# Attention and top-choice expert routing on one core: maxima over experts by pairwise trees, first loads tile by tile on two queues, batch 0's columns as even and odd halves

## The chip, the core and the metric

The kernel runs on one core of a Trainium2 chip. The metric is device time in microseconds (us); the median of several runs counts. Engines are named as the profile names them: PE is TensorE (with PEld, its weight loads), DVE is VectorE, ACT is ScalarE, POOL is GpSimd, and SP is SyncE, which here only issues transfers.

## What is computed

Four batches of `q`, `k`, `v` with 5056 tokens of 256 columns go through an attention over columns, and every output token then goes through one of eight experts.

```python
def _attn_ref(q, k, v, tau):                      # q, k, v: 4 x 5056 x 256
    qn = q / (np.linalg.norm(q, axis=1, keepdims=True) + 1e-06)
    kn = k / (np.linalg.norm(k, axis=1, keepdims=True) + 1e-06)
    s = kn.transpose(0, 2, 1) @ qn / tau          # 256 x 256 for each batch
    s = s - s.max(-1, keepdims=True)
    a = np.exp(s)
    a /= a.sum(-1, keepdims=True) + 1e-09
    return (v @ a).astype(np.float32)

def _moe_ref(x, w_gate, w1, w2):                  # x: 20224 x 256, 8 experts
    cap = N // E                                  # 2528 tokens for each expert
    logits = x @ w_gate
    order = np.argsort(-logits.flatten())
    for idx in order:                             # greedy: best (token, expert) pair first
        tok, e = (int(idx) // E, int(idx) % E)
        if assigned[tok] >= 0 or counts[e] >= cap:
            continue
        assigned[tok] = e
        counts[e] += 1
    for e in range(E):
        mask = assigned == e
        out[mask] = np.maximum(x[mask] @ w1[e], 0.0) @ w2[e]
```

## The kernel before, in words

It has two halves. In the first, for each batch `b`, `scores` (L312) streams `k` and `q` in half chunks of 512 tokens (four token tiles of 128, 512 KB of `k` and as much of `q`) into a ring of four buffers named `ua`. PE adds up `k^T q` over the tokens in one PSUM bank (L338; the trace shows two PE instructions for each of these float32 matmuls), ACT squares each half chunk (L343, L347) and DVE adds the squares (L348). All these loads go through SP's queue; a load waits until PE and ACT are through with the buffer. The very first half chunk is loaded in two pieces for each of `k` and `q`: token tile 0, then tiles 1 to 3 (L323). The constants of the router and `tau` come through ACT's queue (`load_consts`, L485).

After the scores of a batch come its lengths, its softmax (DVE, into `ac`), a transpose (`turned_a`) and `gates` (L427): 16 router columns (2 blocks of 8 experts) are worked out on PE and copied by ACT from PSUM into `ac` (L433), ACT copies `ac` to the buffer from which the value product reads (L436), and DVE copies the 16 columns to a small padded tile `g` (`pads`, L439), from which `logits` (L445) reads its weights. These run between the score matmuls of the next batch. Batch 0 is treated apart: its `ac` is split into a high part `a_hi` (float32r, L436, trace name `a_last`) and a low part `a_f[0]` (L438, trace name `a`), and `value` with `x_tiles_0` (L291, L302) multiplies tokens by both, three float32r matmuls for each 128-row block, 264 columns wide (256 outputs and 8 router columns) in four chunks out of five and 256 wide in the last. There the right-hand operand is read as consecutive columns. The products of batches 1 and 3 are plain float32 matmuls (`x_tiles`, L261). Those of batch 2 are cut into high and low parts again (`x_tiles_cut`, L572, and the feed-forward layers L1489 and L1526): there each right-hand operand lies as all even columns and then all odd columns, and is read alternately from the two halves, `p a m -> p m a`, so that the result keeps its order.

In the second half a small planner writes the order of the instructions of each engine by hand. It keeps a modelled clock for PE and for DVE; the routing of each expert (`route`, L596) is a generator that yields a modelled cost ahead of each instruction, and the planner takes up the next one whose modelled time has come, between the main work's own instructions. The order so made is fixed in the program. `route(p, R)` starts with a maximum of the logits over the `R` experts left (L610, a DVE reduction over a transposed view of `L`, 160 columns for each expert), turns it into a sort key, marks where the maximum stands (L630, L632) and takes a second maximum over the codes of the marks, in bfloat16 (L635). Then it searches a threshold in eight rounds (`compare` L711, `totals` L676 and L689, `hits` L696) in which DVE and PE take turns, and `compact` with `listed` makes the list of the tokens. While the first expert is routed, PE multiplies the values of batches 1 to 3 (the string `TURNS`: F is two plain pairs of token tiles, C is one cut half chunk), then eight late pairs, then the first layer of the first expert. `tend` (L1561) is called behind each pair; once the modelled clock is past the landing of the first expert's weights it hands out one of eight pieces (`split_piece`, ACT L1237 and DVE L1240) in which these weights are split into high and low parts. The split parts go into `ua` buffers, some of which have held cut values until then (`PLACES`, `cleave`).

The feed-forward half then runs `layer1` (PE L1489, ACT L1493, DVE L1498 for the low part `hL` of the hidden layer) and `layer2` (PE L1526, ACT L1535, POOL scatter L1537) expert by expert, with the routing of the next expert woven in.

Of the kernel before, what the change touches and what calls it, by code (L numbers as in the profile page):

```python
# [8 lines left out]
F32 = mybir.dt.float32  # L9
F32R = mybir.dt.float32r  # L10
BF = mybir.dt.bfloat16
# [3 lines left out]
AF = mybir.ActivationFunctionType  # L15
OP = mybir.AluOpType
AX = mybir.AxisListType
# [3 lines left out]
B, N, C = 4, 5056, 256  # L21
E, F = 8, 1024
# [6 lines left out]
COLS = B * NCH * T  # L29
# [4 lines left out]
GW = C + E  # L34
# [8 lines left out]
TH = 4  # L43
# [28 lines left out]
TURNS = "FFCFCFCFCFCFCFCFCFFCFC"  # L72
PLACES = ("ub0", "ub1", "ua0", "ua1", "ub0", "ub1", "vr", "ua0", "ua1", "ua2")
BEHIND = {3: "FF", 4: "C", 5: "CC", 6: "FFFF", 7: "CCC", 8: "CCCC", 9: "FFFFFF"}
CUT = (4, 4, 4, 4, 4)
FIRST_CUT = (2, 4, 4, 4, 4, 2)
PE_TO_DVE = 340
# [26 lines left out]
def attention_moe(ctx: ExitStack, tc: tile.TileContext, q, k, vt, tau, wg, w1t, w2t, tabs, out):  # L104
    nc = tc.nc
    V = nc.vector
    S = nc.scalar
# [56 lines left out]
    for lag in range(2):  # L164
        x = const.tile([128, 1], I32, name=f"px{lag}")
# [37 lines left out]
    L = state.tile([128, E, COLS], F32, name="L0")  # L203
# [31 lines left out]
    a_f = [(apool_l if b == 2 else apool).tile([128, 2, GW], F32 if b else F32R, name=f"a{b}") for b in range(B - 1)]  # L235
    a_hi = apool_l.tile([128, 2, GW], F32R, name="a_last")
    vs = {}
    px_at = [0, True]

    def next_px():  # L240
        px_at[0] += 1
# [31 lines left out]
    with ExitStack() as sctx:  # L273
# [17 lines left out]
        def x_tiles_0(c, t, xs, width):  # L291
            n = 2 if width == C else 1
            px = next_px()
            for i in range(t, t + n):
                y = v_two[c, i - i % 2]
                out_ = px[:, (i - t) * C:(i - t) * C + width]
                j = 0
                for kb in range(2):
                    vH, vL = y[:, 0, kb, i % 2, :], y[:, 1, kb, i % 2, :]
                    aH, aL = a_hi[:, kb, 0:width], a_f[0][:, kb, 0:width]  # L300
                    for l, r in ((vH, aH), (vH, aL), (vL, aH)):
                        newest[0] = PE.matmul(out_, lhsT=l, rhs=r, start=(j == 0), stop=(j == 5))  # L302
                        j += 1
            S.activation(xs[:, t % TH:t % TH + n, 0:width], px[:, 0:n * width].rearrange("p (t c) -> p t c", t=n), AF.Copy)

        pads = []
# [5 lines left out]
        def scores(b, extra):  # L312
            sb = ps_s.tile([128, 512], F32, name="s")
            acc_k = wk.tile([128, TH, C], F32, name="acc_k")
            acc_q = wk.tile([128, TH, C], F32, name="acc_q")
            for c in range(NCH):
                n0 = c * CH
                for h in range(T // TH):
                    kq = big("ua").rearrange("p (a t c) -> p a t c", a=2, t=TH)
                    kt, qt = kq[:, 0], kq[:, 1]  # L320
                    first = c == 0 and h == 0
                    last = c == NCH - 1 and h == T // TH - 1
                    for t0, t1 in ((0, 1), (1, TH)) if b + c + h == 0 else ((0, TH),):  # L323
                        for t_, src in ((kt, k), (qt, q)):
                            if c < NCH - 1:
                                rows = src[b, n0:n0 + CH].rearrange("(p t) c -> p t c", t=T)
                                nc.sync.dma_start(t_[:, t0:t1], rows[:, h * TH + t0:h * TH + t1])
                            elif not last:
                                nc.sync.dma_start(t_, src[b, n0:n0 + HALF_CH].rearrange("(p t) c -> p t c", t=TH))
                            else:  # L330
                                n1 = n0 + HALF_CH
                                n2 = n1 + 128 * (TH - 1)
                                nc.sync.dma_start(t_[:, 0:TH - 1], src[b, n1:n2].rearrange("(p t) c -> p t c", t=TH - 1))
                                nc.sync.dma_start(t_[:REST, TH - 1], src[b, n2:n2 + REST])
                    for t in range(TH):
                        np_ = REST if last and t == TH - 1 else 128
                        for ib in range(2):
                            newest[0] = PE.matmul(sb[:, ib * C:(ib + 1) * C], lhsT=kt[:np_, t, ib * 128:(ib + 1) * 128],  # L338
                                                  rhs=qt[:np_, t, :], start=(first and t == 0 and ib == 0),
                                                  stop=(last and t == TH - 1 and ib == 1))  # L340
                    for t_, acc in ((kt, acc_k), (qt, acc_q)):
                        if first:
                            S.activation(acc, t_, AF.Square)  # L343
                        else:
                            sq = wk.tile([128, TH, C], F32, name="sq", bufs=2)
                            for n, t0, t1 in ((128, 0, TH - 1), (REST, TH - 1, TH)) if last else ((128, 0, TH),):
                                S.activation(sq[:n, t0:t1], t_[:n, t0:t1], AF.Square)  # L347
                                V.tensor_tensor(acc[:n, t0:t1], acc[:n, t0:t1], sq[:n, t0:t1], op=OP.add)  # L348
                    if h == 0:
                        for fn in extra.get((c, "half"), ()):  # L350
                            fn()
                for fn in extra.get(c, ()):
                    fn()
            for acc in (acc_k, acc_q):
                V.tensor_tensor(acc[:, 0:2], acc[:, 0:2], acc[:, 2:4], op=OP.add)
                V.tensor_tensor(acc[:, 0], acc[:, 0], acc[:, 1], op=OP.add)
            pn = pcnt.tile([128, 512], F32, name="pc")
            for i, (acc, ib) in enumerate(((acc_k, 0), (acc_k, 1), (acc_q, 0), (acc_q, 1))):
                newest[0] = PE.matmul(pn[:, i:i + 1], lhsT=acc[:, 0, ib * 128:(ib + 1) * 128], rhs=ones_f[:, 0:1],
                                      start=True, stop=True)  # L360
            nrm = wk.tile([128, 4], F32, name="nrm", bufs=2)
            V.tensor_copy(nrm, pn[:, 0:4])
            return sb, nrm
# [63 lines left out]
        def gates(b, ac, aT):  # L427
            pg = ps_m.tile([128, 512], F32, name="pm")
            for ib in range(2):
                for jb in range(2):  # L430
                    PE.matmul(pg[:, ib * E:(ib + 1) * E], lhsT=aT[:, jb, ib * 128:(ib + 1) * 128],
                              rhs=wg_t[:, jb, :], start=(jb == 0), stop=(jb == 1))
            S.activation(ac[:, :, C:GW], pg[:, 0:2 * E].rearrange("p (i e) -> p i e", i=2), AF.Copy)  # L433
            if b == B - 1:
                a_f.append(apool_l.tile([128, 2, GW], F32, name="a_last"))
            S.activation(a_f[b] if b else a_hi, ac, AF.Copy)  # L436
            if b == 0:
                V.tensor_tensor(a_f[0], ac, a_hi.bitcast(F32), op=OP.subtract)  # L438
            V.tensor_copy(pads[b % 2][:, :, 0:E], ac[:, :, C:GW])  # L439

        def late(fn, *args):
            with tc.issue_after(newest[0].ins):
# [136 lines left out]
    def rtile(name, shape=(128, COLS), dt=F32, bufs=None):  # L579
        t = rt.tile(list(shape), dt, name=name, bufs=bufs)  # L580
        return t

    def ve(n, rate=1, psum=False, ptr=0):
        return "V", ((120 if psum else 58) + n / rate) / 0.96 + 66 * ptr
# [8 lines left out]

    done = {}

    def route(p, R):  # L596
        nonlocal L, L2, U01, asg, ne, ne2
        r = {}
# [7 lines left out]
            es = ne[:, 1, 0:1]  # L606
        else:
            m = rtile("m")
            yield ve(R * COLS)
            V.tensor_reduce(m, L[:, 0:R].rearrange("p r c -> p c r"), axis=AX.X, op=OP.max)  # L610
            key = rtile("t1").bitcast(I32)
            yield ve(COLS, 2)
            V.tensor_scalar(key.bitcast(F32), m, 0.0, None, op0=OP.add)
# [8 lines left out]
            hi = rtile("hi", dt=I16)  # L622
# [2 lines left out]
            klo = rtile("klo", dt=I32)  # L625
            yield ve(COLS, 2)
            V.tensor_scalar(klo, key, 0xffff, None, op0=OP.bitwise_and)
            eq = rtile("eq", (128, E, COLS), BF)
            yield ve(R * COLS)
            V.tensor_tensor(eq[:, 0:R], L[:, 0:R], m[:, None, :].to_broadcast([128, R, COLS]), op=OP.is_equal)  # L630
            yield ve(R * COLS)
            V.tensor_tensor(eq[:, 0:R], eq[:, 0:R], code9[:, 0:R, None].to_broadcast([128, R, COLS]), op=OP.mult)  # L632
            f = rtile("f")
            yield ve(R * COLS)
            V.tensor_reduce(f, eq[:, 0:R].rearrange("p r c -> p c r"), axis=AX.X, op=OP.max)  # L635
            yield ve(COLS)
            V.tensor_tensor(f, f, U01, op=OP.mult)
            Q = R + R % 2
# [143 lines left out]
            t1 = rtile("t1")  # L782
# [50 lines left out]
        if R > 1:  # L833
# [23 lines left out]
            L, L2, ne, ne2 = L2, L, ne2, ne  # L857
# [318 lines left out]
    o = Order()  # L1176
# [371 lines left out]
    with tc.manual_schedule():  # L1548
        o.dve = FIRST_LAT
        plan()  # L1550
        cut_w = [None]
# [8 lines left out]

        def tend():  # L1561
            settle()
            if cut_w[0] and o.pe > cut_w[0][0] and len(cut_w[0]) > 1:
                split_piece(0, *cut_w[0].pop(1))

        def pair(b, c, t):
# [9 lines left out]
        past = ""  # L1576
# [5 lines left out]
        for kind in TURNS:  # L1582
# [8 lines left out]
            else:  # L1591
                k = past.count("C")
                b, c, h = cloven[k]
# [37 lines left out]
        for p in range(E):  # L1631
# [32 lines left out]
            h = {}  # L1664
# [98 lines left out]
```

## Time and profile before

| | us |
|---|---|
| median of 3 runs | 1224.33 (1223.97 to 1225.0) |
| the profiled execution | 1227.58 |
| its span on the core | 1225.6 |
| PE busy | 1201.0 (98%) |
| PE weight loads busy | 1096.6 (89%) |
| DVE busy | 870.0 (71%) |
| ACT busy | 581.0 (47%) |
| POOL busy | 408.0 (33%) |

A row of the timeline gives the start, the time from the start of its first instruction to the end of its last, the engine and line, output and inputs, how often, and in brackets the idle time of the engine ahead of it with what ended it. Matmuls overlap: one lasts far longer than the distance to the next, so the distance is read from rows that hold many. A row of a list of waits gives who waited on whom, the sum, how many times, and the longest. A row of the windows gives, for a stretch, each engine's busy time and how many instructions, then the granted PE clock, the DMA engines' busy share and what they moved in GB/s. A row of the chain gives the start, the time, and what stood on the chain.

### The profile page before, as it was taken

The page shows a single profiled execution, that of the slowest core. Times are in us where ns is not written, and L with a number is a line of the kernel's source. Part 1 is how long each engine was busy: PE and PEld are TensorE (multiplying, and loading weights), DVE is VectorE, ACT ScalarE, POOL GpSimd, SP SyncE. Part 2 cuts the span into 40 slices and gives each one's busy share as a digit, 9 for nine tenths or more (in the row PEclk, how much of TensorE's full clock was granted, in tenths as well). Part 3 has the DMA queues.
Part 4 walks back from the last instruction along what each step waited for, and adds up shares of the span by engine and source line. Part 5 has one row for each costly group of instructions (what it writes and reads, how often), then busy time and mean ns, then how long its engine had stood idle before and what let it go on. Part 6 is the DMA issues. An engine that isn't in the chain of part 4 may idle for free.

```text
span 1225.6 us, 23691 instructions
## 1 busy us (share of the span) xinstructions
PE 1201.0 (98%) x8885; PEld 1096.6 (89%) x8885; DVE 870.0 (71%) x2410; ACT 581.0 (47%) x1322; POOL 408.0 (33%) x655
## 2 busy tenths in 40 slices
PE   7999999999999999999999999999999999999997
PEld 6889977798899989899988999999999999999997
DVE  6688696789888878888888888797765453444430
ACT  5657644555434443345354454354455544344331
POOL 1000001110442462344434444444444444443422
PEclk9999999999999999999999999999999999999999
DMA  8998996795333122313422243243234233422310
GB/s 298 354 401 307 405 318 213 171 241 207 121 103 120 58 93 74 134 57 116 147 81 83 75 152 113 82 131 128 86 108 159 86 116 124 142 94 98 103 65 34
DMA packets 69970, 183.82 MB, mean 150 GB/s; under 512 B 11104, under 2 KB 33760, under 8 KB 65248
## 3 DMA queue, kind: packets, MB, share of 16 engines
q1 hardware_dynamic: 39808, 97.54, 22.3%
q0 software_dynamic: 20656, 63.72, 17.6%
q10 hardware_dynamic: 9392, 21.06, 4.5%
q8 instruction: 69, 1.13, 0.4%
q14 instruction: 45, 0.37, 0.1%
HBM read 122.77 MB, written 59.24 MB: 149 GB/s over the span
## 4 chain that ended last, share of the span: by engine, by line
PE 83%; DVE 8%; issue 4%; POOL 2%; DMA 1%; ACT 1%; POOLq 0%; another core or an unknown queue 0%; SPq 0%; DVEq 0%; ACTq 0%
PE ph L1489 31%; PE py L1526 29%; PE s L338 9%; PE px L261 4%; PE pc L676 3%; PE px L302 2%; PE px L572 2%; PE px L450 1%; POOL out_dram L1537 1%; DVE acc_q L348 1%; DVE acc_k L348 1%; DMA ua<-in_q_dram 1%; DVE ge L711 0%; PE pi L916 0%; DVE f L635 0%
## 5 line engine op out<-in xcount | busy, mean ns | idle before, releaser
L1526 PE MATMUL py<-ua,hH 128*128 128x256 f32 (+1 forms) x2560 | 438.7, 277 | 0.0
L1489 PE MATMUL ph<-xH,ua 128*128 128x512 f32 (+3 forms) x1312 | 394.4, 376 | 3.7 <-DVE hL L1498 3.6
L1526 PEld LDWEIGHTS py<-ua,hH 128*128 128x128 f32 (+1 forms) x2560 | 389.5, 190 | 1.7
L1526 PE MATMUL py<-ua,hL 128*128 128x256 f32 (+1 forms) x1280 | 352.7, 276 | 0.0
L1498 DVE SCALAR_TENSOR_TENSOR hL<-ph,hH 128x512 fp32r<-128x512 f32 (+3 forms) x328 | 217.1, 664 | 109.3 <-ACT hH L1493 97.6
L1493 ACT ACTIVATE hH<-ph 128x512 fp32r<-128x512 f32 (+3 forms) x328 | 191.0, 583 | 202.1 <-PE ph L1489 188.1
L1489 PEld LDWEIGHTS ph<-xH,ua 128*128 128x128 f32 x1312 | 244.8, 189 | 34.6 <-DVE hL L1498 6.2
L1537 POOL DMA_INDIRECT out_dram<-y,idx x160 | 164.4, 1027 | 294.7 <-ACT y L1535 248.2
L1489 PE MATMUL ph<-xL,ua 128*128 128x512 f32 (+3 forms) x656 | 245.4, 374 | 0.5 <-DVE xL L1431 0.5
L1526 PEld LDWEIGHTS py<-ua,hL 128*128 128x128 f32 (+1 forms) x1280 | 243.9, 191 | 0.0
L1259 POOL DMA_INDIRECT xg<-x_d,src x160 | 164.0, 1025 | 93.1 <-issue 52.7
L1535 ACT ACTIVATE y<-py 128x256 f32<-128x256 f32 (+1 forms) x160 | 61.5, 385 | 261.8 <-PE py L1526 204.3
L338 PE MATMUL s<-ua 128*128 128x256 f32 (+1 forms) x640 | 144.9, 385 | 7.1 <-DMA ua<-in_q_dram 7.1
L338 PEld LDWEIGHTS s<-ua 128*128 128x128 f32 (+1 forms) x640 | 121.7, 193 | 26.8 <-issue 6.7
L1489 PEld LDWEIGHTS ph<-xL,ua 128*128 128x128 f32 x656 | 124.2, 189 | 14.6 <-DVE xL L1431 1.5
L347 ACT ACTIVATE sq<-ua 128x1024 f32<-128x1024 f32 (+1 forms) x80 | 76.4, 970 | 51.3 <-DMA ua<-in_k_dram 17.1
L1357 DVE TENSOR_TENSOR xL<-xT,xH 128x256 fp32r<-128x256 f32 (+1 forms) x136 | 50.5, 420 | 58.2 <-ACT xH L1353 57.8
L1270 POOL COPY spacer<-hH 1x1 f32<-1x1 f32 x110 | 24.1, 219 | 158.9 <-ACT hH L1493 148.9
L368 POOL TENSOR_SCALAR ny<-ny 128x4 f32<-128x4 f32 x4 | 2.0, 506 | 182.6 <-ACT ny L367 182.6
L1240 DVE TENSOR_TENSOR ua<-ub,ua 128x512 fp32r<-128x512 f32 x64 | 47.1, 745 | 13.6 <-ACT ua L1237 12.7
L1353 ACT ACTIVATE xH<-xT 128x256 fp32r<-128x256 f32 (+1 forms) x136 | 52.3, 449 | 3.2 <-DMA xT<-via 2.9
L348 DVE TENSOR_TENSOR acc_k<-acc_k,sq 128x1024 f32<-128x1024 f32 (+2 forms) x40 | 44.2, 1112 | 7.9 <-ACT sq L347 6.7
(337 smaller groups left out, 1424.5 us busy)
## 6 DMA issues: line engine op xcount, KB each, us to landing
x_d<-xs ACTq DMA_DIRECT2D x40, 512.0 KB
ua<-in_k_dram SPq DMA_DIRECT2D x35, 512.0 KB
ua<-in_q_dram SPq DMA_DIRECT2D x35, 512.0 KB
via<-xs SPq DMA_DIRECT2D x33, 512.0 KB
xT<-via SPq DMA_DIRECT2D x132, 128.0 KB
vr<-in_vt_dram SPq DMA_DIRECT2D x14, 1024.0 KB
ua<-in_vt_dram SPq DMA_DIRECT2D x4, 1024.0 KB
ua<-in_vt_dram POOLq DMA_DIRECT2D x5, 512.0 KB
```

Of the source, the lines that this page charges most:

```text
L338: newest[0] = PE.matmul(sb[:, ib * C:(ib + 1) * C], lhsT=kt[:np_, t, ib * 128:(ib + 1) * 128], rhs=qt[:np_, t, :], start=(first and t == 0 ...
L347: S.activation(sq[:n, t0:t1], t_[:n, t0:t1], AF.Square)
L348: V.tensor_tensor(acc[:n, t0:t1], acc[:n, t0:t1], sq[:n, t0:t1], op=OP.add)
L1259: P.indirect_dma_start(out=xg[:n, i, :], out_offset=None, in_=rows, in_offset=bass.IndirectOffsetOnAxis(ap=routed[p]["src", col][:n, col:c ...
L1353: S.activation(hi[:, a], rows[:, a], AF.Copy)
L1357: V.tensor_tensor(lo[:, a], rows[:, a], hi[:, a].bitcast(F32), op=OP.subtract)
L1489: PE.matmul(ph[:, 0:nt], lhsT=l[:, w], rhs=in_turn(x_, kb, nt).rearrange("p a m -> p m a"), start=(i == 0), stop=(i == 5))
L1493: S.activation(hH[:, fb, 0:nt], ph[:, 0:nt], AF.Relu)
L1498: V.scalar_tensor_tensor(hL[:, fb, 0:nt], ph[:, 0:nt], 0.0, hH[:, fb, 0:nt].bitcast(F32), op0=OP.max, op1=OP.subtract)
L1526: PE.matmul(py[:n, 0:C], lhsT=l[:, fb, tk], rhs=w, start=(j == 0), stop=(j == 23))
L1535: S.activation(y[:n], py[:n, 0:C], AF.Copy)
L1537: sd = P.indirect_dma_start(out=out, out_offset=bass.IndirectOffsetOnAxis(ap=routed[p]["idx", col][:n, col:col + 1], axis=0), in_=y[:n], i ...
```

## The change

1. The two maxima over the experts in `route` become trees of pairwise maxima (`largest`): the upper half of the experts against the lower half, then again, an odd one taken along in an instruction of its own. Each instruction is its own step for the planner.
2. The first half chunk is loaded token tile by token tile, `k` by SP's queue and `q` by ACT's.
3. Batch 0's high and low parts are written as even and odd columns (`apart`) and read alternately.
4. ACT copies the router columns to `pads` straight from PSUM, ahead of its copy of `ac`; DVE's copy is gone.
5. `tend` hands out a piece of the first expert's first weight only when nine cut half chunks are past, of its second when ten are (`FREED`).

```diff
+FREED = (9, 10)
+    def apart(a):
+        return a.rearrange("p k c -> p (k c)").rearrange("p (a k m) -> p a k m", a=2, k=2)
@@ x_tiles_0
-                    aH, aL = a_hi[:, kb, 0:width], a_f[0][:, kb, 0:width]
+                    aH, aL = (apart(a)[:, :, kb, 0:width // 2].rearrange("p a m -> p m a") for a in (a_hi, a_f[0]))
@@ scores
-                    for t0, t1 in ((0, 1), (1, TH)) if b + c + h == 0 else ((0, TH),):
+                    at_head = b + c + h == 0
+                    for t0, t1 in [(t, t + 1) for t in range(TH)] if at_head else ((0, TH),):
                         for t_, src in ((kt, k), (qt, q)):
                             if c < NCH - 1:
-                                nc.sync.dma_start(t_[:, t0:t1], rows[:, h * TH + t0:h * TH + t1])
+                                (nc.scalar if at_head and src is q else nc.sync).dma_start(t_[:, t0:t1], rows[:, h * TH + t0:h * TH + t1])
@@ gates
-            S.activation(ac[:, :, C:GW], pg[:, 0:2 * E].rearrange("p (i e) -> p i e", i=2), AF.Copy)
+            for to in (ac[:, :, C:GW], pads[b % 2][:, :, 0:E]):
+                S.activation(to, pg[:, 0:2 * E].rearrange("p (i e) -> p i e", i=2), AF.Copy)
-            S.activation(a_f[b] if b else a_hi, ac, AF.Copy)
             if b == 0:
-                V.tensor_tensor(a_f[0], ac, a_hi.bitcast(F32), op=OP.subtract)
-            V.tensor_copy(pads[b % 2][:, :, 0:E], ac[:, :, C:GW])
+                hi, lo = (apart(a).rearrange("p a k m -> p k m a") for a in (a_hi, a_f[0]))
+                in_turn_ = ac.rearrange("p k (m a) -> p k m a", a=2)
+                S.activation(hi, in_turn_, AF.Copy)
+                V.tensor_tensor(lo, in_turn_, hi.bitcast(F32), op=OP.subtract)
+            else:
+                S.activation(a_f[b], ac, AF.Copy)
+    def largest(to, x, tmp, n):
+        while n > 1:
+            h = n // 2
+            yield ve(h * COLS)
+            V.tensor_tensor(to[:, None] if n == 2 else tmp[:, 0:h], x[:, 0:h], x[:, n - h:n], op=OP.max)
+            if n % 2:
+                yield ve(COLS)
+                V.tensor_tensor(to if n == 3 else tmp[:, 0], tmp[:, 0], x[:, h], op=OP.max)
+            x, n = tmp, h
@@ route
-            yield ve(R * COLS)
-            V.tensor_reduce(m, L[:, 0:R].rearrange("p r c -> p c r"), axis=AX.X, op=OP.max)
+            eq = rtile("eq", (128, E, COLS), BF)
+            yield from largest(m, L, eq.bitcast(F32).rearrange("p r c -> p (r c)").rearrange("p (r c) -> p r c", c=COLS), R)
-            eq = rtile("eq", (128, E, COLS), BF)
-            yield ve(R * COLS)
-            V.tensor_reduce(f, eq[:, 0:R].rearrange("p r c -> p c r"), axis=AX.X, op=OP.max)
+            yield from largest(f, eq, eq, R)
@@ tend
-            if cut_w[0] and o.pe > cut_w[0][0] and len(cut_w[0]) > 1:
+            if cut_w[0] and o.pe > cut_w[0][0] and len(cut_w[0]) > 1 and past.count("C") >= FREED[cut_w[0][1][0]]:
                 split_piece(0, *cut_w[0].pop(1))
```

## Rows read from the trace of the kernel before

**Rows 1.** The page: busy time, share of the span and instructions of each engine.
```profile
PE 1201.0 (98%) x8885; PEld 1096.6 (89%) x8885; DVE 870.0 (71%) x2410; ACT 581.0 (47%) x1322; POOL 408.0 (33%) x655
```
**Rows 2.** What PE waited for between 400 and 700 us.
```profile
PE ph L1489 <- DVE hL L1498: 3.6, 3, 1.3
```
**Rows 3.** Timeline of PE, the first 45 us: the score matmuls of batch 0.
```profile
4.08 2.05 PE L338 MATMUL s<-ua 128*128 128x256 f32 x4 [4.08 <-DMA ua<-in_q_dram]
9.12 35.71 PE L338 MATMUL s<-ua 128*128 128x256 f32 x156 [2.99 <-DMA ua<-in_q_dram]
```
**Rows 4.** Timeline of all engines, the first 20 us: constants, second half chunk, buffers freed.
```profile
5.92 0.17 DVE L488 RECIPROCAL scale<-tau_t 128x2 f32<-128x2 f32 x1 [4.24 <-DMA tau_t<-in_tau_dram]
...
11.40 1.23 DVE L348 TENSOR_TENSOR acc_k<-acc_k,sq 128x1024 f32<-128x1024 f32 x1 [2.26 <-ACT sq L347]
11.59 1.06 ACT L347 ACTIVATE sq<-ua 128x1024 f32<-128x1024 f32 x1
...
13.64 0.33 SPq L327 DMA_DIRECT2D ua<-in_k_dram  x1
...
17.09 0.33 SPq L327 DMA_DIRECT2D ua<-in_k_dram  x1
```
**Rows 5.** Windows of the head: all engines, then PE clock, DMA share, GB/s.
```profile
3.50:4.00 0.50, 0.00 (x0) 0.00 (x0) 0.00 (x0) 0.00 (x0) 0.30 (x1) 1.00 0.05 0
...
9.00:10.00 1.00, 0.88 (x2) 0.82 (x3) 0.14 (x2) 0.93 (x1) 0.00 (x0) 1.00 1.05 430
```
**Rows 6.** The chain: runs of matmuls, consecutive columns (L302) and alternating halves (L1526).
```profile
97.57 5.82 PE px L302 x48
...
136.63 5.61 PE px L302 x48
...
988.41 10.72 PE py L1526 x96
```
**Rows 7.** Timeline around batch 0's gates: high part (ACT), low part (DVE).
```profile
81.63 0.65 ACT L436 ACTIVATE a_last<-ac 128x528 fp32r<-128x528 f32 x1
...
83.05 0.70 DVE L438 TENSOR_TENSOR a<-ac,a_last 128x528 fp32r<-128x528 f32 x1
```
**Rows 8.** Timeline at the end of batch 2: when transfers land, when PE comes to batch 3.
```profile
146.94 1.06 ACT L347 ACTIVATE sq<-ua 128x1024 f32<-128x1024 f32 x1 [0.70 <-DMA ua<-in_q_dram]
...
151.08 1.11 PE L338 MATMUL s<-ua 128*128 128x256 f32 x4
```
**Rows 9.** Timeline of batch 3's gates: ACT's copy, DVE's copy, PE's wait.
```profile
215.50 0.18 ACT L433 ACTIVATE ac<-pm 128x16 f32<-128x16 f32 x1 [0.36 <-PE pm L431]
...
217.26 0.13 DVE L439 COPY g<-ac 128x16 f32<-128x16 f32 x1
...
217.59 0.67 PE L261 MATMUL px<-a_last,ua 128*128 128x256 f32 x2 [1.16 <-DVE g L439]
```
**Rows 10.** Timeline of three reductions over experts, and PE's next waits on DVE.
```profile
292.69 2.11 DVE L610 TENSOR_REDUCE m<-L 128x160 f32<-128x1120 f32 x1
...
297.01 0.59 PE L916 MATMUL pi<-E__97,G 128*128 128x162 bf16 x6 [0.55 <-DVE G L906]
...
410.09 1.84 DVE L635 TENSOR_REDUCE f<-eq 128x160 f32<-128x960 bf16 x1
...
415.45 0.36 PE L1489 MATMUL ph<-xH,ua 128*128 128x224 f32 x1 [1.29 <-DVE hL L1498]
...
515.22 1.52 DVE L610 TENSOR_REDUCE m<-L 128x160 f32<-128x800 f32 x1
...
517.33 0.38 PE L916 MATMUL pt<-E__97,G 128*128 128x162 bf16 x3 [1.46 <-DVE ext L1031]
```
**Rows 11.** Timeline of two-operand DVE instructions: float32, and 16-bit in and out.
```profile
236.29 1.48 DVE L711 TENSOR_TENSOR ge<-hi,th 128x1200 bf16<-128x1200 int16 x2
...
278.50 0.32 DVE L786 TENSOR_TENSOR asg<-asg,Gf 128x160 f32<-128x160 f32 x1
```
**Rows 12.** Timeline: the first expert's weights are split, fifth of eight pieces.
```profile
301.74 0.69 ACT L1237 ACTIVATE ua<-ub 128x512 fp32r<-128x512 f32 x1 [0.96 <-PE px L572]
```

## The prediction

> **What bounds the kernel now.** I read the busy shares first: PE works 98% of the span and no other engine over 71% [rows 1]. PE's order is fixed in the program, so a part of the change is worth what it takes out of PE: idle time in which PE waits, or matmuls that come too slowly. Then I read PE's waits stretch by stretch, the timeline around each, and the chain. What PE loses lies in a few places. At the head, PE does token tile 0 at 4.08 and then stands for 2.99 us until `q` of tiles 1 to 3 has landed [rows 3]. Behind that pause it is also slow: the rest of the first half chunk, 12 instructions from 9.12 to the issue at 13.64 that waits for its buffer, takes 4.52 us, while the 16 of the next take 17.09 - 13.64 = 3.45 us, 0.216 each [rows 3, 4]. So 1.9 us (4.52 - 12 x 0.216) go to matmuls at nearly half pace behind idle time, though the granted clock reads 1.00, the upper level (2.4 GHz), in that stretch [rows 5]. In batch 3's gates PE stands 1.16 us for DVE's small copy [rows 9]. Between 290 and 520 us it stands 0.55, 1.29 and 1.46 us for DVE work that came behind a reduction over experts [rows 10]; its waits on `hL` from 400 to 700 are 3.6 us in three [rows 2]. Elsewhere it streams, so time is won only by a denser stream.
>
> **Part by part.**
>
> *First loads.* PE no longer waits for three tiles at once. What ends last next is the second half chunk: ACT begins to square its `q` at 11.59 without waiting for a transfer, so it had landed by then [rows 4]. If it lands as before and PE is through with the first half chunk by then, PE ends the second at 11.59 + 3.45 = 15.04 instead of 17.09: 2.05 us gained. PE has the time: from 4.08, 16 instructions at 0.216 and the 1.9 us of slow start end at 9.4 if tiles come in time, and by 11.3 with 1.9 us more. Bounds: at best the second half chunk lands by 9.4, and 17.09 - (9.4 + 3.45) gives 4.2. At worst PE stands so long ahead of 11.59 that it starts slowly again: 2.05 - 1.9 gives 0.15. The DMA engines moved nothing from 3.5 to 4.0 and 430 GB/s at full share from 9 [rows 5], so there is room for earlier bytes, but I have no row of four loads at once and take 2.0. A later first tile (three more 128 KB pieces beside it are 0.79 MB for `k` and `q`, 1.8 us at 430 GB/s) would only eat slack ahead of 11.59. On ACT's queue the four issues stand ahead of those of the constants, at 0.33 us each (an SP issue in [rows 4]) some 1.3 us. DVE waits for `tau` until 5.92 and has 2.26 us of idle time before its first sum at 11.40 [rows 4]; that covers it, and without the cover ACT's squares would come late, not PE. Behind 17 us PE sets the pace of the loads (each waits for its buffer), so the gain is kept.
>
> A rule of the Trainium skill speaks against the second queue (DMA: Bandwidth & Descriptors, section "Issuing engines are not separate DMA queues"): transfers from several engines share the same 16 DMA engines, and a second issuing engine saves only issue time. By it the bytes come as before and the sum keeps the 2.0; without it, it would have the 4.2.
>
> *Even and odd columns.* `x_tiles_0` has 240 matmuls: 192 of 264 columns at 5.82/48 = 0.1213 us and 48 of 256 at 5.61/48 = 0.1169. The second layer, read alternately, does 256 columns in 10.72/96 = 0.1117 [rows 6]; eight columns more in proportion make 0.1152. The gain is 192 x 0.0061 + 48 x 0.0052 = 1.4 us if batch 0 follows. Its halves lie 1056 bytes apart, not 1024 as elsewhere; if that matters, nothing is gained. I take 1.4, the row of the same reading. Loads hide behind PE in this stage: a transfer that ACT squares at 146.94 belongs to batch 3, which PE begins at 151.08 [rows 8]; 4.1 us of slack against 1.4. Without it the transfers would keep the 1.4.
>
> Against this stands the note on SBUF "cachelines" (the Trainium skill, SBUF — State Buffer, section "Door 1"): accesses that stay in a 16-byte line run at full bandwidth, and each step to another line pays. By it alternating halves is the slow way. The trace disagrees: the alternating run is the faster [rows 6].
>
> *Batch 0's gates.* One more ACT copy, 0.18 us [rows 9], stands ahead of the high part. That ended at 81.63 + 0.65 = 82.28, and DVE was busy until 83.05 before the low part [rows 7], so 0.77 us cover the copy and a slower strided write. Without the cover it costs 0.2. I take 0.
>
> *Batch 3's router columns.* ACT's copy into `g` follows the one at 215.50 and ends near 215.9 instead of 217.26 + 0.13 = 217.39 [rows 9]. PE's wait of 1.16 goes; the copy of the whole of `a`, which now starts 0.18 later, may stand last for that matmul instead. I take 1.0, bounds 0.5 to 1.2. For batches 1 and 2 nobody waited on that copy: 0.
>
> *Trees.* Two-operand float32 instructions take 0.32 us for 160 elements and 1.23 for 1024 [rows 4, 11]: 0.15 + 1.05 ns for each element. For seven experts the tree is 480, 160, 160, 160: 0.65 + 3 x 0.32 = 1.61 against 2.11. For five it is 320, 160, 160: 0.49 + 2 x 0.32 = 1.13 against 1.52. For six, 480 and three of 160, 1.61 against about 1.84 for the first maximum. The second maximum is 16-bit, and 1200 elements in 0.74 [rows 11] is about half the time for each: some 1.2 against 1.84. So DVE is 0.5 us earlier at PE's wait of 0.55, 0.2 + 0.65 earlier at that of 1.29, and 0.4 at that of 1.46 [rows 10]: 0.5 + 0.85 + 0.4 = 1.75. At best smaller steps let the awaited work in between, and all 3.3 go. At worst it is a loss: the planner's costs change (for six experts from 1060 to 1241 ns for each maximum, by its formula) and there are more steps to weave, so orders shift from the second expert on, and new waits of the size of these appear; three of them would make it -2. For the first expert the search goes in turns with PE, whose places are fixed, so an earlier start is mostly waited off. I take 1.7.
>
> *`FREED`.* ACT stood 0.96 us at 301.74 for matmuls that still read the buffer [rows 12]; its later copies come earlier, worth at most that on PE. I take 0.3. The pieces move by one or two pairs of tiles; ACT is 47% busy [rows 1].
>
> The sum: 2.0 + 1.4 + 0 + 1.0 + 1.7 + 0.3 = 6.4 us. The profiled execution took 1227.58 (2 us around its span), so it would take 1221.2; the median lies 3.25 lower, 1224.33, and becomes 1217.9.
>
> **The rivals.**
>
> - *The head gives 4.2*, because pieces on two queues use the time in which the DMA engines stood still [rows 5]: 1224.33 - 8.6 = 1215.7. For it: the idle half microsecond. Against it: the shared engines.
> - *The head gives 0.15*, because PE stands until 11.59 and starts slowly again, as it did at 9.12 [rows 3]: 1219.8.
> - *Alternating does not help at 1056 bytes*: 1219.3; or each change of half costs PE as much as it was to gain: 1220.7. Against both: [rows 6]. The second is what the Trainium skill's note (SBUF — State Buffer) would do here.
> - *The new order spoils the second half.* For it: DVE's list is full there, and PE's three waits on `hL` of 1.2 us [rows 2] show how dearly a late low part is paid. The trees' gain goes, and the other parts give 4.7. Each new wait costs 1.2: with two to five of them we are within 0.2% of before. It turns to slower by over 0.2% (2.45 us, about what a measurement of this kernel can tell from no change) beyond (4.7 + 2.45)/1.2, some six new waits, one in every second of the twelve trees of experts two to seven: 1226.8 and above.
> - *The trees do nothing where PE waits*, because the releaser was other work: 1219.6; inside the forecast's range.
>
> **How the numbers follow.** Chances: the forecast, with smaller misses of the trees in it, 0.46; the head at 4.2, 0.18; the head at 0.15, 0.15; alternating without effect 0.03 and slower 0.02; a spoiled order within 0.2% 0.12, and slower 0.04. Faster by over 0.2% is everything down to 1221.9: 0.84; within 0.2%: 0.12; slower: 0.04. The range: all best ends together are 4.2 + 1.4 + 1.2 + 3.3 + 0.3 = 10.4, 1213.9; I begin at 1213.5. Upward it reaches to 1222.3, which leaves out most of the spoiled orders.
>
> **What would show it.** In the changed profile PE's score matmuls of batch 0 run from about 4 us with no pause of 3 us, and the second half chunk's buffer is freed near 15 instead of 17.09. 48 matmuls of `x_tiles_0` take 5.5 us, not 5.82. Batch 3's gates show no PE wait on DVE's copy. The maxima are DVE two-operand instructions of 0.3 to 0.8 us, and the waits at 297, 415 and 517 are shorter or gone. I am wrong if the head's gain is given back before 45 us, if a transfer ends PE's waits between 80 and 200 us, or if PE's waits on DVE from 320 us on sum up to more than before.

## The result, and the profile after

| | before | after |
|---|---|---|
| median of 4 runs each | 1224.51 us | 1213.63 us |
| profiled execution, span | 1227.58, 1225.6 us | 1213.0, 1211.1 us |

The ratio is 0.9912 (95% interval 0.990 to 0.9925): 10.9 us less, where 6.4 were forecast. The two traces differ by 14.5 us, because the traced execution of before lay some 3 us above its median. So a gain read from the traces is too large in sum, most of all behind 240 us, where most of that execution's waits stand.

The page of after, busy times (before: [rows 1]):
```profile
PE 1195.4 (99%) x8885; PEld 1095.1 (90%) x8885; DVE 863.6 (71%) x2428; ACT 580.8 (48%) x1326; POOL 407.8 (34%) x655
```
PE does the same 8885 matmuls in 5.6 us less of busy time, and its idle time falls from 24.6 to 15.7 us (span minus busy). DVE has more instructions and 6.4 us less work.

The chain of work that ended last, of after (start, length, what):
```profile
95.59 5.40 PE px L306 x48
133.82 5.36 PE px L306 x48
175.40 14.21 PE s L343 x64
234.80 2.59 PE px L265 x12
340.00 7.17 PE ph L1506 x33
537.51 7.39 PE ph L1506 x34
674.08 8.71 PE ph L1506 x40
973.88 10.72 PE py L1543 x96
```
The same pieces of work begin in the chain of before at 97.57, 136.63, 178.45, 240.26, 346.87, 548.79, 688.03 and 988.41. After is ahead by 2.0 us, then 2.8, 3.05, 5.46, 6.87, 11.28, 13.95 and 14.53. So 3 us come before batch 0's values are through, 2.4 in batch 3's gates, and the rest in the half with the search, nearly all of it up to 690 us; nothing is given back behind that. Not all of it need be the change's. Between 430 and 480 us after gains 2.25 us on this trace of before, where PE waits for a low part of the hidden layer; in a second trace of after (the second set below) the wait is there again. PE's timeline of before, then PE's waits in that second trace from 420 to 708 us:
```profile
447.84 0.48 PE L1489 MATMUL ph<-xH,ua 128*128 128x512 f32 x1 [1.30 <-DVE hL L1498]
```
```profile
PE ph L1506 <- DVE hL L1515: 1.2, 1, 1.2
```
The second trace gains nothing on before from 430 to 480 us. So this wait comes and goes in one and the same kernel, and it may be most of the 3.6 us by which the difference of the traces exceeds that of the medians.

The head of after, PE's timeline and SP's issues (before: [rows 3, 4]):
```profile
5.67 11.62 PE L343 MATMUL s<-ua 128*128 128x256 f32 x40 [5.67 <-DMA ua<-in_q_dram]
11.89 0.33 SPq L332 DMA_DIRECT2D ua<-in_k_dram  x1
15.34 0.33 SPq L332 DMA_DIRECT2D ua<-in_k_dram  x1
```
PE begins later (5.67, not 4.08), stands no more, and frees the second half chunk's buffer at 15.34, not 17.09. It is still slow at first: its first sixteen instructions end at the issue at 11.89, after 6.22 us, the next sixteen take 3.45.

The timelines of before and then of after between 71 and 84 us (batch 0's parts in before: [rows 7]):
```profile
73.68 0.62 DVE L414 TENSOR_SCALAR ac<-nf,sm 128x256 f32<-128x256 f32 x2
74.18 0.72 PE L422 MATMUL pm<-ident,ac 128*128 128x128 f32 x4 [0.18 <-DVE ac L414]
74.21 1.22 DVE L348 TENSOR_TENSOR acc_q<-acc_q,sq 128x1024 f32<-128x1024 f32 x1
83.81 0.39 PE L302 MATMUL px<-a,v_two 128*128 128x264 f32 x1 [0.60 <-DVE a L438]
```
```profile
71.77 0.17 DVE L416 RECIPROCAL sm<-sm 128x2 f32<-128x2 f32 x1
71.86 1.20 DVE L353 TENSOR_TENSOR acc_q<-acc_q,sq 128x1024 f32<-128x1024 f32 x1
72.98 0.61 DVE L419 TENSOR_SCALAR ac<-nf,sm 128x256 f32<-128x256 f32 x2
73.47 0.72 PE L427 MATMUL pm<-ident,ac 128*128 128x128 f32 x4 [0.92 <-DVE ac L419]
74.03 3.62 PE L343 MATMUL s<-ua 128*128 128x256 f32 x16
82.12 0.38 PE L306 MATMUL px<-a_last,v_two 128*128 128x264 f32 x1
82.34 0.28 PE L306 MATMUL px<-a,v_two 128*128 128x264 f32 x1
```
New here is the wait of 0.92 for `ac`: a sum of 1.20 us stands ahead of it on DVE, which stood behind it in before. The wait for the low part `a`, 0.60 in before, is gone.

Batch 3's gates, PE's timeline, of before (between them stands [rows 9]) and then of after:
```profile
215.39 1.05 PE L450 MATMUL px<-ua,g 128*32 128x512 f32 x2
218.19 3.20 PE L450 MATMUL px<-ua,g 128*32 128x512 f32 x26
```
```profile
212.34 3.62 PE L459 MATMUL px<-ua,g 128*32 128x512 f32 x28
```
The same 28 matmuls, and two others, took from 215.39 to 221.39 us; without the wait they run in one stretch of 3.62. Of the 2.4 us gained, the row of the wait holds 1.16. The loss is larger than that row, which begins only where the last matmul has ended: from the start of the pair at 215.39 to the start of the next at 217.59 are 2.20 us, where two matmuls at the 0.12 of the 26 behind them come in 0.24.

PE's waits in after from 274 to 706 us (who, for whom: us, times, longest); and DVE's first tree, for eight experts:
```profile
PE pt L933 <- DVE ext L1048: 0.8, 1, 0.8
PE pc L913 <- DVE cb L907: 0.7, 1, 0.7
PE pt L1442 <- DMA xg<-x_d,src: 0.3, 1, 0.3
PE ph L1506 <- DVE hL L1515: 0.3, 1, 0.3
```
```profile
219.28 0.82 DVE L609 TENSOR_TENSOR eq<-L 128x640 f32<-128x640 f32 x1
220.13 0.49 DVE L609 TENSOR_TENSOR eq<-eq 128x320 f32<-128x320 f32 x1
220.66 0.32 DVE L609 TENSOR_TENSOR m<-eq 128x160 f32<-128x160 f32 x1
```
In before the same stretch of the program has 8.2 us of waits, 3.6 of them for `hL` [rows 2], 1.46 at the one for `ext` [rows 10]. After has 2.1 here; its second trace has 6.2 (276 to 708 us), 2.1 of them for `Ex` and 1.7 for `hL`.

### The profile page after: what moved, and what is told of

Its sections match the earlier page's. It is cut to its first block, busy times and chain, and to the rows that moved or that the text cites. A ratio compares the mean times of both kernels' runs of the same rounds, so it can differ in the third digit from the quotient of the medians.

```text
span 1211.1 us, 23720 instructions
## 1 busy us (share of the span) xinstructions
PE 1195.4 (99%) x8885; PEld 1095.1 (90%) x8885; DVE 863.6 (71%) x2428; ACT 580.8 (48%) x1326; POOL 407.8 (34%) x655
## 4 chain that ended last, share of the span: by engine, by line
PE 88%; DVE 4%; issue 4%; POOL 2%; DMA 1%; ACT 0%; POOLq 0%; SPq 0%; ACTq 0%; DVEq 0%
PE ph L1506 32%; PE py L1543 31%; PE s L343 9%; PE px L265 5%; PE pc L693 2%; PE px L306 2%; PE px L581 2%; PE px L459 1%; POOL out_dram L1554 1%; DMA ua<-in_q_dram 1%; DVE acc_k L353 1%; DVE acc_q L353 1%; PE pi L933 1%; PE pt L933 0%; DVE nf L410 0%
## 5 line engine op out<-in xcount | busy, mean ns | idle before, releaser
L1554 POOL DMA_INDIRECT out_dram<-y,idx x160 | 162.3, 1015 | 292.8 <-ACT y L1552 239.1
L353 DVE TENSOR_TENSOR acc_k<-acc_k,sq 128x1024 f32<-128x1024 f32 (+2 forms) x40 | 44.2, 1112 | 10.4 <-ACT sq L352 9.5
```

What stands on the lines that cost most here:

```text
L1554: sd = P.indirect_dma_start(out=out, out_offset=bass.IndirectOffsetOnAxis(ap=routed[p]["idx", col][:n, col:col + 1], axis=0), in_=y[:n], i ...
```

## The experiments

Three sets of four kernels ran, each set on one chip beside runs of the kernel before, whose medians there were 1230.99, 1231.53 and 1223.97 us; every time below is to be read against the one of its set.

**First set: the parts by themselves.** Each is the kernel before with some hunks of the change.

*Trees and `FREED`* (the hunks of `largest`, `route` and `tend`):
```
+            yield from largest(m, L, eq..., R)
+            yield from largest(f, eq, eq, R)
+            if ... and past.count("C") >= FREED[cut_w[0][1][0]]:
```


> The kernel before with the maxima as trees and the FREED bound, and nothing else of the change (the trees stand with FREED in every kernel here). Theory S, the prediction's sum: 1.7 + 0.3 = 2.0 us less than before. Rival O, the second half carries the surplus: of the 10.9 us by which the medians differ, the traces put 1.45 before the end of the head and some 4.0 into the even/odd columns and batch 3's gates, so 5.5 us remain for what is done here. Rival P: the trees gain the whole 9 us by which the two traces differ behind 240 us. Rival N, the parts help each other: below 1 us alone. In its trace S wants waits of PE shortened at three places between 290 and 520 us; O wants new places of gain behind 430 us, in the runs of feed-forward matmuls.

Measured: 1224.58, ratio 0.9948 (0.993 to 0.9966): 6.4 us less. Three times theory S, and by the median nearest to O. PE's waits in this kernel, 280 to 720 us:
```profile
PE ph L1505 <- DVE hL L1514: 1.2, 2, 0.7
PE pt L932 <- DVE ext L1047: 0.8, 1, 0.8
PE pc L705 <- DVE Dr L698: 0.7, 1, 0.7
```
With four smaller ones they sum to 4.8 us, against 8.2 in before; the largest part, 2.4, went from the waits for `hL`. Two of before's three stand behind reductions: that of 1.29 at 415 [rows 10], and one of 0.98 that the prediction did not list, some 3 us after the second of two reductions over four experts:
```profile
614.49 1.27 DVE L635 TENSOR_REDUCE f<-eq 128x160 f32<-128x640 bf16 x1
618.72 0.48 PE L1489 MATMUL ph<-xH,ua 128*128 128x512 f32 x1 [0.98 <-DVE hL L1498]
```
The third is the one at 447.84. The trace of trees with `FREED` is ahead of that of before by 0.5 us at 240, 1.6 at 318, 2.3 at 415, 2.8 at 517, 4.2 at 619 and 3.9 at the end. So the trace places some 4 of the 6.4 us; that trace of before took 1227.58 us, 3.4 less than before's median in this set, and where the rest comes from is not shown.

*`FREED` alone* (the last of these lines).

> The kernel before with the FREED bound alone: ACT's pieces of the first expert's weight split wait until the ninth or tenth pair of that kind is through. Theory S: 0.3 us less than before, 0.96 at most. Rival O: the 1.1 us that the trace of after is ahead between 282 and 318 us are this part's. Rival N: nothing alone, since it is there only to go with the trees; or a loss of up to 1 us, when pieces crowd behind 300 us.

Measured: 1231.57, ratio 1.0001 (0.9988 to 1.0015). It is worth nothing by itself. Trees without it were not run, so the 6.4 belong to the trees as they stand with it.

*Columns alone* (even and odd halves, and the router columns by ACT).

> The kernel before with batch 0's halves as even and odd columns and the router columns of every batch copied by ACT, and nothing else. Theory S: 1.4 + 0 + 1.0 = 2.4 us less than before. Rival O: 4.0 us, as the trace of after shows it: 48 matmuls of x_tiles_0 in 5.40 us instead of 5.82 (0.42 times 4 and 0.25 make 1.9, of which some 0.3 is given back to other waits), and 2.4 us in batch 3's gates, since the runs of matmuls on either side of the wait of 1.16 us become denser too. Rival N: batch 0's longer high and low parts (1.15 and 1.07 us instead of 0.65 and 0.70) cost PE some 1 us when the head has not made room ahead of them: 1.4 to 3.0.

Measured: 1228.0, ratio 0.9976 (0.9963 to 0.999): 3.0 us less. Its trace has no wait of PE in batch 3's gates, and by its marks 2.4 us come there, as by O; batch 0's values give 1.2, and 0.35 are lost again ahead of them, 0.23 of it at the wait for `a` (0.83 us, 0.60 in before).

*The head alone* (tile by tile, `q` by ACT's queue).

> The kernel before with the first half chunk's tiles loaded one by one, q by ACT's queue, and nothing else. Theory S: 2.0 us less than before (between 0.15 and 4.2), with the second half chunk's buffer freed at 15.0. By the trace of after: PE begins at 5.67 instead of 4.08 and the buffer is freed at 15.34, so 1.75, of which 1.45 is still there at 45 us. Rival G: the gain is given back between 73 and 84 us, where PE waits for ac 0.9 us instead of 0.2 in after: 0.7 us in all.

Measured: 1229.95, ratio 0.9991 (0.9979 to 1.0003). By its trace it is 0.94 us ahead at 45 us and level with before at 84: PE stands again at the head, 1.36 us at 11.49, and waits 1.9 us for `ac`. In the trace rival G held, and more strongly than it said; by the medians the gain is 1.0, and an interval that holds 1 decides nothing. The kernels with trees, columns and head, which hold all of the change between them, sum to 10.4 us, so by the medians the parts neither help nor hinder each other much.

**Second set: what of the trees gains, and what the waits cost.** Each is after with one thing altered; the first is after itself.

> The changed kernel as it is, beside the kernel before on the same chip, as the mark for the three that follow. Theory C (clock): where the kernel before stands for DVE in batch 3's gates and near 437 us, the granted clock behind the wait falls from 1.00 to 0.50 for 3.4 and 7 us in some executions; after has neither wait, so its times lie within 1.5 us of each other and its trace has no clock below 1.00 ahead of the end, on a chip too where the kernel before shows such stretches. Where before takes 1231 us, after then takes 1215 to 1218, 13 to 16 us less. Theory S: the difference is 10.9 on any chip, made of waits and matmul durations alone.

Measured: 1221.7 (1219.13 to 1222.4), ratio 0.9913 (0.9889 to 0.9937), 9.8 us less. Theory C falls: the gain is the same in proportion whether before takes 1224.51 or 1231.53, and after too has an execution in which the granted clock falls, behind its new wait. The windows (us; PE, PEld, DVE, ACT, POOL busy, granted clock, share of the DMA engines, GB/s) and PE's timeline there:
```profile
75.32 1.07 PE L427 MATMUL pm<-ident,ac 128*128 128x128 f32 x4 [2.39 <-DVE ac L419]
76.19 4.91 PE L343 MATMUL s<-ua 128*128 128x256 f32 x16
```
```profile
74.00:76.00 2.00, 0.68 (x4) 0.66 (x5) 2.00 (x4) 1.66 (x2) 0.00 (x0) 0.84 1.02 382
76.00:78.00 2.00, 2.00 (x7) 1.64 (x6) 1.71 (x2) 1.57 (x4) 0.00 (x0) 0.50 1.00 401
```
The wait is 2.39 us here, 0.92 in the first trace of after. Behind it 16 score matmuls take 4.91 us at a granted clock of 0.50; at 1.00 they took 3.62 in the first trace of after.

*Trees as one step of the planner:*
```
+        yield ve(n * COLS)
         while n > 1:
             h = n // 2
-            yield ve(h * COLS)
```


> After, with all instructions of a tree under one step of the planner, at the cost of the reduction that they replace. Twelve trees keep their DVE durations; what is gone is the finer weaving. Theory D (DVE time): the 7.4 us that DVE is quicker (20.6 us in 14 reductions, 13.25 us in 36 tree instructions) make the gain, so this takes what after takes, within 0.5 us. Theory W (weave): the small steps let the low parts in between, so this loses 2 to 4 us, and waits of 0.5 us and more for hL come back between 290 and 530 us.

Measured: 1221.95, as after, with runs of 1220.49 to 1224.15. Theory D holds, and the loss of 2 to 4 us of theory W is not seen: what counts is not that small steps let other work in.

*The old reduction in the trees' order:*
```
             yield ve(h * COLS)
-            V.tensor_tensor(...)
...
+        V.tensor_reduce(to, x.rearrange("p r c -> p c r"), axis=AX.X, op=OP.max)
```


> After, with every engine's order kept as the trees made it, and the old reduction over experts standing where the last instruction of each tree stood: order without the shorter DVE work. Theory D (DVE time): loses 3 to 4 us against after, most of what the trees gained in the trace of the kernel with trees and FREED alone (3.9 us), by waits of PE near 290, 395 to 405 and 505 us. Theory W (order): within 0.7 us of after.

Measured: 1227.69, ratio 0.9971 (0.9953 to 0.9988): 6.0 us above after, with every engine's order that of after but for the maxima themselves; its runs (1223.95 to 1231.91) all lie above after's. So it is the 7.4 us of shorter DVE work (20.6 us in 14 reductions, 13.25 in 36 tree instructions) that carry the gain. How much of them comes through is less sure: 6.0 and 6.4 us by the two pairs of medians, 4.7 by the traces of this kernel and of after in this set (what after gains on it behind 240 us), some 4 by the trace of trees with `FREED`. PE's waits in this kernel, 276 to 420 and 420 to 708 us:
```profile
PE ph L1505 <- DVE src L1007: 1.0, 1, 1.0
PE pc L692 <- DVE ge L727: 0.9, 2, 0.6
PE pi L932 <- DVE ext L969: 0.7, 1, 0.7
```
```profile
PE ph L1505 <- DVE hL L1514: 2.0, 2, 1.3
PE ph L1505 <- DVE k L993: 1.3, 1, 1.3
```
PE waits for `src`, `k`, `ge`: things that DVE makes long after the maximum. The reading is that the time which the reduction takes too long goes down DVE's list to the next thing that PE needs.

*Router columns by DVE again:*
```
-            for to in (ac[:, :, C:GW], pads[b % 2][:, :, 0:E]):
+            for to in (ac[:, :, C:GW],):
...
+            V.tensor_copy(pads[b % 2][:, :, 0:E], ac[:, :, C:GW])
```


> After, with the router columns copied by DVE from ac again, as before; trees, even and odd columns, FREED and the head stay. Theory S: PE's wait of 1.16 us in batch 3's gates comes back, at about 210 us, and costs 1.0 to 1.2 us. Theory C (clock): in executions in which the granted clock falls to 0.50 behind that wait, some 3.4 us long, another 1.7 us are lost; the times then spread over 3 us or more, and the median is 1.5 to 3 us above after's.

Measured: 1223.13 (1220.77 to 1224.16), 1.4 us above after, with overlapping times: between the 1.2 of theory S and the 1.5 of theory C, and it decides neither. In its trace the wait is back, with the fall of the clock:
```profile
217.44 1.09 PE L265 MATMUL px<-a_last,ua 128*128 128x256 f32 x2 [1.16 <-DVE g L449]
218.46 4.42 PE L460 MATMUL px<-ua,g 128*32 128x512 f32 x26
```
```profile
218.00:220.00 2.00, 2.00 (x10) 0.40 (x12) 0.00 (x0) 0.00 (x0) 0.00 (x0) 0.50 0.97 175
```
The 26 matmuls take 4.42 us; in the trace of before, behind the same wait at clock 1.00, 3.20. The fall costs 1.2 us here and comes in some executions.

**Third set: the head.** Again after, altered.

*One queue* (`q` of the first half chunk by SP, as `k`):
```
-  (nc.scalar if at_head and src is q else nc.sync).dma_start(...)
+  nc.sync.dma_start(...)
```


> After, with the first half chunk's q pieces on SP's queue too: eight pieces tile by tile on one queue. Theory S (the engines' share sets the landing): PE's first score matmul comes within 0.5 us of after's 5.7 and the second half chunk's buffer is freed within 0.3 us of after's 15.3. Theory Q (the second queue matters): the eight issues of 0.33 us each behind each other put the second half chunk's loads 1.3 us later and the buffer is freed at 16.0 to 16.7. In both, ACT's and DVE's orders fall back to those of before around 40 to 75 us: the square root of the norms stands behind work that waits for PE and not for a load, DVE's last sum ahead of `ac` goes behind it, and PE waits for `ac` 0.2 to 0.5 us, not 0.9 to 2.4, with no fall of the clock there.

Measured: 1213.35 (1212.92 to 1214.52), ratio 0.9916 (0.9902 to 0.9929). Timelines of PE and SP, and PE's waits from 40 to 140 us:
```profile
4.34 6.32 PE L343 MATMUL s<-ua 128*128 128x256 f32 x16 [4.34 <-DMA ua<-in_q_dram]
11.43 5.85 PE L343 MATMUL s<-ua 128*128 128x256 f32 x26 [0.77 <-DMA ua<-in_q_dram]
15.19 0.33 SPq L332 DMA_DIRECT2D ua<-in_k_dram  x1
```
```profile
PE px L306 <- DVE a L446: 1.0, 1, 1.0
PE px L306 <- ACT xs L308: 0.5, 1, 0.5
PE pm L427 <- DVE ac L419: 0.2, 1, 0.2
```
The buffer is freed at 15.19 (15.46 in after's trace of this set): theory S, though its other half fails, for PE begins at 4.34 and not near 5.7, and then stands 0.77 us for the second half chunk. The second queue does not free the buffer earlier, in agreement with the Trainium skill (DMA: Bandwidth & Descriptors, "Issuing engines are not separate DMA queues"). With one queue the old order comes back and the wait for `ac` is 0.2 us, so that PE keeps 1.9 us on before, about the 2.0 of the forecast, up to 74 us. But it then reaches batch 0's `a` earlier and waits 1.0 there, and at 84 us it is 1.5 us ahead of before, as after is.

*Tile 0's `q` by SP* (`... and src is q and t0`).

> After, with tile 0's q issued by SP right behind its k, and the q of tiles 1 to 3 by ACT's queue. Theory A (order around ac): the head's gain of 1.4 us at 45 us is kept, PE's wait for `ac` falls to 0.2 to 0.5 us, and the clock does not fall behind it: 0.5 to 1 us less than after where its clock holds, 1.5 to 3 us less in the median on a chip where it falls. Rival: the wait for `ac` stays, since DVE and not the order is what is late: same as after. Also: tile 0's pair lands first, so PE begins nearer to 4.1 than to 5.7; by itself that is worth nothing, since later tiles end last.

Measured: 1215.52 (1214.42 to 1216.07), no faster than after; PE begins at 5.72, against what was said. The wait for `ac` is 0.2 and that for `a` 1.0, as in the one before; its trace also has the granted clock at 0.62 and 0.52 from 192 to 194 and to 196 us, behind a wait of 0.40 for `acc_k`. Every engine's order is that of the one-queue kernel, though two queues are in use: it is the order, and not the second queue as such, that lengthens the wait for `ac`. And at this order the second queue gains nothing: the median is 2.2 us above that of one queue. Theory A has the wait right and its price wrong: most of it moves on to `a`.

*Without the head's part* (`((0, 1), (1, TH))`, by SP).

> After, without the part at the head: tile 0 and then tiles 1 to 3, all by SP, as before. Theory S: 1.5 to 2.0 us slower than after. Theory A: the head's 1.45 us are mostly given back at `ac`, and behind that wait the clock falls in some executions, so that the head is worth between +0.7 us and a loss of 1.5 us: this kernel is then as fast as after or faster, and its times are the closer ones, where every other wait of over 1 us is gone.

Measured: 1215.47 (1214.62 to 1219.04). *After once more:*

> The changed kernel as it is, on the chip of the three others, as their mark. By theory A its trace shows a wait for `ac` of 0.9 to 2.4 us at 73 to 75 us, and its times spread over more than those of the two kernels in which that wait is short.

Measured: 1214.73 (1213.8 to 1217.31), with a wait of 1.15 us for `ac`. The head is worth 0.7 us by medians, less than these can tell apart. One queue lies 1.4 us below after, with intervals that overlap (0.9902 to 0.9929, 0.9919 to 0.9946): it is no worse by these, and simpler. Its runs (1212.92 to 1214.52) all lie below those without the head's part, so what there is to gain at the head seems to come from loading tile by tile, and not from the second queue.

## Why the prediction was right, step by step

Faster was right, and what was said to bound the kernel, PE's waits and the distance of its matmuls, holds. The size was not: the time lies in the range by 0.13 us. Its low end was made, among others, from a head of 4.2 us and trees of 3.3; the head gave less and the trees more, and that the two fitted was luck. The sum was 4.5 us short. Trees, batch 3 and batch 0's gates gave more than forecast, the first loads and `FREED` less.

- *Trees: 1.7 forecast, 6.0 to 6.4 measured by medians, some 4 placed by the trace.* The step that failed is the list of places: I took the reductions' saving only at the three waits of [rows 10] that stand close behind one. There the trace with trees and `FREED` gains 0.9, 0.8 and 0.7, against 0.5, 0.85 and 0.4. But DVE is busy for 86% of 240 to 620 us (326 of 380 us in the windows of before), so a reduction's lost time can be passed on until PE meets it at an `hL` or `ext`. Of the `hL` waits [rows 2] I counted only the one at 415 and put all three under the rival of a spoiled order; the one at 618.72, behind the reductions over four experts, was left out, and 1.0 us came there. The bound of 3.3 was too low as well: it held seven, six and five experts only. The first expert (4.8 us to 2.8) I had "mostly waited off"; the trace is 0.5 us ahead there. The tree for six experts I miscounted: it is 480, 160 and 160 elements, 1.30 us in the trace of after and not 1.61, so that the planner's cost for it falls (1060 to 1015 ns by its formula) where I had it rise.
- *Batch 3's router columns: 1.0 forecast, 2.4 measured in the traces of after and of the columns alone (1.4 by the medians of the second set).* The row of the wait held 1.16; I did not measure from the start of one matmul to the start of the next (2.20 us for two), though [rows 3, 5] had shown such a loss beside idle time at the head, nor did I count the fall of the clock behind it in some executions.
- *First loads: 2.0 forecast, 1.45 at 45 us, 0.7 behind `ac`.* The buffer was freed at 15.34 (15.04 forecast), but not by the step I gave: the transfer of the second half chunk did not end last. PE did, which was through with the first at 11.89 and not by 11.3, 0.3 us behind my 11.59, and went on without a wait. The reciprocal of `tau`, for which I had 1.3 us behind the 5.92 of before, stands at 14.88 in after; PE did not wait for it. What cost more stands in none of my steps: other issue times made the program's generator order ACT's and DVE's work otherwise, and a DVE sum of 1.2 us came ahead of `ac`. The square root of the norms now stands behind a square that waits for a load.
- *Even and odd columns: 1.4 forecast, 1.6 measured (1.47 ahead at 84 us, 3.05 at 178; 1.2 in the trace of the columns alone).* 48 matmuls of 264 columns take 5.40, not 5.82 [rows 6] (5.5 forecast), 1056 bytes apart or not. The note on cachelines (the Trainium skill, SBUF — State Buffer, "Door 1") would have made them slower; the trace disagrees again.
- *Batch 0's gates: 0 forecast, 0.7 gained, but not by my reason.* The cover held: in after the high part ends at 80.64, and DVE is busy until 81.0. What I left out is that the low part takes 1.07 us and not 0.70 (the high one 1.15, not 0.65), and that it starts only when DVE is through. PE does not meet that in after, since it comes later, through `ac`; where `ac` is early, PE waits 1.0 for `a`, against 0.6 in before.
- *`FREED`: 0.3 forecast, 0 measured.*

With the measured terms, 6.2 + 2.4 + 0.7 + 1.6 + 0.7 make 11.6, against 10.9; the first is of medians, the others of traces. Of the rivals none came true as told: the head did not give 4.2; in after PE did not stand again as the 0.15 wanted (it did in the trace of the head alone, and by medians the head's 0.7 cannot be told from 0.15); alternating halves were not slower; and the new order did not cost what the trees gained.

## What to carry to other kernels

Where an engine off the critical path is 86% busy, as here, with ordered work that the bounding engine consumes, price a saving on it well above the waits that stand right behind it: here those gave 1.75 us, the saving was 7.4, and 4 to 6.4 came through. Price an idle gap of TensorE from start to start of the matmuls around it, and not by its row: here 2.20 us, of which two matmuls need 0.24, held a row of 1.16. After moving a load, look at the order of the other engines before you count the gain.

## What the hardware showed

- The granted clock fell from 1.00 to 0.50, the lower level (1.2 GHz), behind gaps of PE of 0.40 us (at 191, in tile 0's `q` by SP), 1.16 (at 217, in the head alone, `FREED` alone and router columns by DVE), 2.07 (at 128, without the head's part), 2.39 (at 75, in the second set's after) and 2.60 us (at 437, in `FREED` alone), for some 3 to 7 us. Behind the same 1.16 us it stayed at 1.00 in the traces of before and of trees with `FREED`, and so it did behind 2.24 us (at 75, in router columns by DVE) and 2.51 us (at 430, in the trees as one step). What decides it from one execution to the next stays open.
- Some executions have a wait of 2.1 to 2.6 us for `Ex` (ending at 437 us in `FREED` alone, at 659 in the second set's after, at 430 and 661 in the trees as one step), with DVE idle for 4 us ahead of it though PE's counting matmuls had ended; it comes with trees and without. Its cause stays open. Such waits, and that for `hL` near 445 us, may be part of why one trace of a kernel can lie 3 us off its median.
- Eight pieces of 128 KB on two queues let PE begin at 5.15 to 5.80 us in eight traces, on one queue at 4.34 in the one trace there is. PE then stood 0.77 us for the second half chunk with one queue; with two it stood 1.36 us in the head alone, 0.85 in router columns by DVE, and under 0.3 in the other six.
